# A product by seven block products for eight in two more pairs of feature blocks, with the order of the units written anew

## The chip, the cores and the metric

The kernel runs on one core of one Trainium2 chip. The metric is the device time of one execution in microseconds (us). Five engines work side by side, each through a queue of its own that it serves in order: TensorE (PE in the profile; PEld is its weight loads), VectorE (DVE), ScalarE (ACT), GpSimd (POOL) and SyncE (SP), which here only issues DMAs. The engines meet only at semaphores.

## The reference: what is computed

```python
# q, k, v: (4, 8, 768, 64); lam: (8,); blocks of 64 tokens, state kv carried from block to block
intra = ((qb @ kb.T) * Dmask) @ vb
inter = (qb * lam_pow) @ kv_state
out[block] = intra + inter
kv_state = lam**64 * kv_state + (kb * rev_pow).T @ vb
...
x = out.transpose(0, 2, 1, 3).reshape(3072, 512)
h = x @ w_in            # 512 -> 2048
g = np.maximum(0.01 * h, h)
y = g @ w_out           # 2048 -> 512
```

Everything is float32 to begin with (the launch hands the two weight matrices over as float64).

## The kernel before, in words

**Three passes for one product.** Each float32 operand is split into three parts, high, low and middle (`h`, `l`, `m`), and each product is three matmuls on TensorE. So an activation needs one ScalarE pass (`h`) and two VectorE passes (`l`, `m`) before TensorE can use it.

**Tokens and features.** The 3072 tokens are 24 chunks of 128; four chunks are a group of 512 tokens (six groups, `g` = 0 to 5), and two groups are a pair of groups (`pr` = 0, 1, 2). The 2048 features are 8 pairs of blocks of 128 (`p` = 0 to 7).

- *Attention* of chunk `c` is a round: `round_of` (transposes, `scores`, `outputs`), line 328 for its small matmuls, 418 for its transposes. It writes the group's `X[g % 2]`.
- *Weights in*: `w_in(p)` (line 639) loads 1 MB, puts float32 together from the two words (lines 603 to 610) and splits it (line 612) into `W[p]`.
- *Up*: `up(g, p)` (line 704) is X times `W[p]`: two blocks of 12 matmuls of 512 columns (line 716). ScalarE scales the bank between the second and third pass (line 734) and then applies the leaky ReLU into one of two `gs` buffers (line 739). From there the result goes to DRAM, as `G` (line 745) or, where the seven-product form is used, as `BB`: then `sums` (line 767) also makes three sums of quarters on VectorE, 128x256 each (line 773), and stores six quarter blocks for four (line 781), through a spare buffer that `spare` names (line 757).
- *Weights out*: `w_out` and `w_out_parts` bring `W_out` and put it in the place of `W[p]` after the last group's `up`; `w_sums(p)` (line 677) makes the sums of the weights' quarters that the seven-product form needs.
- *Out*: the activations come back from DRAM as *units* of 512 KB in a ring of five slots (`unit`, line 799): load on SP's queue (line 815), `h` on ScalarE (818), `l` and `m` on VectorE (821, 825). TensorE uses a unit in one of two ways. `plain(pr, p, gi)` (line 868) is 24 matmuls (line 841) for one group and one pair of feature blocks, into four banks. `strassen(pr, t, u)` (line 844) is 12 matmuls for block product `t` of seven, for a pair of groups and two pairs of feature blocks (`u`). Seven such units stand for eight times 12 matmuls. The price is in other places: unit 4 takes two loads and one more VectorE pass (833), and partial results are copied (`copy_banks`, 943) and added (`add_banks`, 948 and 949) between the accumulating banks X, Y, V and Z (two banks each).

**Before**, pairs of groups 1 and 2 use the seven-product form for `p` = 0 to 3 (`NS = 4`, two `u`), and pair 0 is all `plain`.

**The order.** The list `seq` (line 951 on) holds steps in order of rank. `Plan.add` takes each operation with an assumed cost, what it reads and writes, and that rank. `Plan.emit` (line 83) lists them: of all operations that are ready, it takes the one that can start earliest by the assumed costs, and among equals the one of lower rank. So an operation of TensorE that is ready goes ahead of one of lower rank that is late. Each engine's queue is then fixed in that order. `LEAD` puts the load and the split of a unit 8 steps ahead of its matmuls. The ring's first seven units use slots 0, 1, 4, 0, 1, 2, 3 (`slots`, line 797): 0 and 1 lie in `X[0]`, 2 and 3 in `X[1]`, which the last group's `up` reads, and 4 lies in `raws`.

Of the kernel before, what the change touches and what calls it, by code (L numbers as in the profile page):

```python
# [36 lines left out]
class Plan:  # L37
# [7 lines left out]
    def __init__(self):  # L45
        self.ops, self.last, self.rank = [], {}, 0.0
        self.chain, self.chains = None, {}
        self.warm, self.slack, self.more = 0.0, 0.0, {}
        self.first = {"PE": 0.0, "ACT": 0.0, "DVE": 3.4, "POOL": 0.0, "DMA": 0.2}
        self.cold, self.idle, self.spare = 6.0, None, None  # L50
# [10 lines left out]
    def add(self, eng, us, fn, reads=(), writes=(), rank=0.0):  # L61

        n, deps = len(self.ops), set()
        for k in reads:
            w, r = self.last.setdefault(k, [None, []])
            if w is not None:
                deps.add(w)
            r.append(n)
        for k in writes:
            w, r = self.last.setdefault(k, [None, []])  # L70
            if w is not None:
                deps.add(w)
            deps.update(r)
            self.last[k] = [n, []]
        deps.discard(n)
        ways = {eng: us} if isinstance(eng, str) else dict(zip(eng, us))
        if self.slack:
            self.more[n] = self.slack
        if self.chain is not None:
            self.chains[self.chain].append(n)  # L80
        self.ops.append((ways, fn, deps, (self.rank + rank, n), set(writes)))

    def emit(self):
# [30 lines left out]
        while len(done) < n:  # L114
            best = None
            for e in free:
                for i in able[e]:
                    if e == "PE" and (i != locked[0] if locked else i in follows):
                        continue
                    t = max(free[e], since(i, e))  # L120
                    if (best is None or (t, self.ops[i][3]) < best[:2]) and good(i, e, t):
                        best = (t, self.ops[i][3], i, e)
            t, _, i, e = best
            ways, fn = self.ops[i][:2]
# [38 lines left out]
def kernel(  # L163
# [10 lines left out]
    nc = tc.nc  # L174
# [23 lines left out]

    NS = 4
    LEAD = 8.0  # L200
    WSLACK = 5.0
    DV = 10
# [36 lines left out]
    KINDS_B = ("1", "7", "2", "3", "5", "6")  # L239
    BB = [[dram.tile([P, 6 * 2 * T], F32, name=f"b{r}_{u}", tag=f"b{r}_{u}") for u in range(NS // 2 if r else 0)] for r in range(NG // 2)]  # L240
    G = [{p: dram.tile([P, 4 * T], F32, name=f"g{r}_{p}", tag=f"g{r}_{p}") for p in range(NS if r else 0, NP)} for r in range(NG // 2)]


    NA = 9120
    att = sb([P, NA], "att")
    used = 0
# [7 lines left out]
    ident = part(P)  # L254
    kqv_f = [part(2 * H * D + (TURN - 2) * HP * C * (i == 1)) for i in range(3)]
    kqv = [[x[:, i * H * D:(i + 1) * H * D].rearrange("p (h d) -> p h d", h=H) for i in range(2)] for x in kqv_f]
# [389 lines left out]
    ATT = ["fk", "fq", "sc"] + [f"{x}{i}" for x in ("k", "q", "v", "kT", "qT", "qsT") for i in range(2)] + [f"st{i}" for i in range(4)]  # L646
    staging = [w32f, lowt.bitcast(F32), gs[1].rearrange("p f t -> p (f t)")]
# [3 lines left out]

    def free_attention():
        extra["att"] = sb([P, NA], "att", F32R)

# [9 lines left out]
    def more(z, p):  # L664
        a, n = (p * 3 + z) * 3 * NQ, 3 * NQ
        return extra["att"][:, a:a + n] if a + n <= NA else extra["lows"][:, :n]

# [36 lines left out]
    def up(g, p, lo=0, hi=GC):  # L704
# [20 lines left out]
        for fs in blocks:  # L725
            kb = ("b10", "b2")[n_b % 2] if n_b < 0 else ("b10", "b11", "b2")[n_b % 3]
# [6 lines left out]
            ns = 0.6 if len(fs) * n == T else 0.4  # L733
            add("ACT", ns, lambda b=b: nc.scalar.activation(out=b, in_=b, func=AF.Copy, bias=0.0, scale=S + 1.0), [], [kb], rank=-1.5)  # L734
            for i, f in enumerate(fs):
                add("PE", us, lambda f=f, d=b[:, i, :]: product(d, f, 2), keys("m"), [kb])
            for i, f in enumerate(fs if p < NS and g > 1 else [None]):
# [19 lines left out]
    def spare(g, p):  # L757

        r = raws.rearrange("p (i n) -> p i n", i=NRAW)
        if g == NG - 1:  # L760
            x, i = (kTs, qTs)[p // 2], p % 2
            return x[i].rearrange("p y t -> p (y t)").rearrange("p (i t) -> p i t", i=2), f"{'kq'[p // 2]}T{i}"
        if p % 2:
            return lows[1].bitcast(F32).rearrange("p (i t) -> p i t", i=2), "low1"
# [79 lines left out]
    def strassen(pr, t, u, lead):  # L844
# [20 lines left out]
        add("PE", 0.227 * 12, go, [f"r{z}{j}" for z in "hlm"] + [f"{'w' if w >= 0 else 'e'}{z}{p}" for z in "hlm" for p in ps_],  # L865
            ACC[d])

    def plain(pr, p, gi, lead, last=False, banks=None):
# [9 lines left out]
        def go(fs, cs, lo=0, n=T):  # L878
            for f in fs:
                for c in cs:  # L880
                    d, i = BANKS[gi][c]
                    product(acc[d][i][:, lo:lo + n], j, f * T + lo,
                            lambda z, f=f, c=c: W[p][z][:, f * 2 * NQ + c * P:f * 2 * NQ + (c + 1) * P], first=pr == p == f == 0, n=n)

# [60 lines left out]
    def add_banks(d, s):  # L945
        for i in range(2):
# [3 lines left out]

    seq = [("a", 0), ("a", 1), ("a", 2), ("a", 3), ("wi", 1), ("b", 4), ("r", 4), ("up", 0, 1), ("wi", 0), ("r", 5),
# [4 lines left out]
    nxt, n_out, begin = 3 * GC, 0, len(seq)  # L956
    ORDER = [4, 0, 5, 1, 6, 2, 7, 3]
    steps = [(g, p) for g in range(2, NG) for p in (ORDER if g < NG - 1 else range(NP))]

    def key_of(g, p):  # L960
        return f"G{g}{p}00" if p >= NS else f"B{g}{p}"

    for n, (g, p) in enumerate(steps):
# [10 lines left out]
        if g == NG - 1:  # L974
            seq.append(("wp", p))
            if p == NS - 1:
                seq.append(("fr",))
    for pr in range(NG // 2):
# [11 lines left out]
        else:  # L990
            i = seq.index(("up", NG - 1, NP - 1))
            seq[i:i] = [n(0, 0)]
            seq += [n(0, 1), n(1, 0), n(1, 1), ("ws", 0), n(2, 0), n(2, 1), ("ws", 1), n(3, 0), n(3, 1), ("ws", 2), n(4, 0), n(5, 0), ("ws", 3), n(6, 0), n(7, 0)]
    seq += [n(p, 1) for p in range(NS, NP - 2)] + [("end", NG // 2 - 1, 1, NP - 2)]

    freed = False
    for n, x in enumerate(seq):
# [9 lines left out]
        elif x[0] == "wi":  # L1007
            w_in(x[1])
        elif x[0] == "up":
            up(*x[1:])  # L1010
        elif x[0] == "wo":
            w_out(*x[1:])
        elif x[0] == "wp":
            if not freed:
                add("DVE", 0.0, lambda: None, [], ["psc", "po", "X0", "X1", "Z0", "Z1"])
                freed = True
            w_out_parts(x[1])
        elif x[0] == "ws":
            if x[1] == 0:
                add("DVE", 0.0, free_attention, [], ATT + [f"e{z}{p}" for z in "hlm" for p in range(NS)])  # L1020
            w_sums(x[1])
        elif x[0] == "fr":
            add("ACT", 0.0, free_raws, [], [f"raw{i}" for i in range(NRAW)] + ["rh4", "rl4", "rm4", "zr"])
        elif x[0] == "s":
            strassen(*x[1:], LEAD)
        elif x[0] == "n":
            plain(*x[1:], LEAD)
        elif x[0] == "copy":
# [38 lines left out]
```

## Time and profile before

| | |
|---|---|
| median of 3 runs | 600.31 us (599.99 to 600.97) |
| the profiled execution | 600.87 us |
| its span (first to last instruction) | 599.1 us |
| TensorE busy, instructions | 588.3 us, 5346 |
| VectorE / ScalarE / GpSimd busy | 393.8 / 290.6 / 132.3 us |
| granted TensorE clock | 1.000 |
| DMA | 119.89 MB, mean 200 GB/s |

The profile's times are from the span's start. Its parts that are used here: the busy time of each engine in stretches of 10 us; the list of who waited for whom; the time line of one engine (start, duration, line, operation, how often; in brackets the idle time before it and what ended it); and the mean duration of groups of instructions.

### The profile page before, as it was taken

The page shows a single profiled execution, that of the slowest core. Times are in us where ns is not written, and L with a number is a line of the kernel's source. Part 1 is how long each engine was busy: PE and PEld are TensorE (multiplying, and loading weights), DVE is VectorE, ACT ScalarE, POOL GpSimd, SP SyncE. Part 2 cuts the span into 40 slices and gives each one's busy share as a digit, 9 for nine tenths or more (in the row PEclk, how much of TensorE's full clock was granted, in tenths as well). Part 3 has the DMA queues.
Part 4 walks back from the last instruction along what each step waited for, and adds up shares of the span by engine and source line. Part 5 has one row for each costly group of instructions (what it writes and reads, how often), then busy time and mean ns, then how long its engine had stood idle before and what let it go on. Part 6 is the DMA issues. An engine that isn't in the chain of part 4 may idle for free.

```text
span 599.1 us, 13248 instructions
## 1 busy us (share of the span) xinstructions
PE 588.3 (98%) x5346; PEld 487.3 (81%) x5346; DVE 393.8 (66%) x534; ACT 290.6 (49%) x459; POOL 132.3 (22%) x170
## 2 busy tenths in 40 slices
PE   7899999999999999999999999999999999999997
PEld 6678888888888888888788888888888888888886
DVE  4999783434375664465279849876678695788752
ACT  3678975445555555565587744431344233252210
POOL 2554660554657374230000000000000000000000
PEclk9999999999999999999999999999999999999999
DMA  9899864795979999886678636436467546384533
GB/s 209 217 274 253 241 185 123 176 242 145 240 240 254 243 261 258 256 234 226 211 271 310 227 100 208 153 101 180 136 174 247 177 141 187 129 253 169 176 106 70
DMA packets 162797, 119.89 MB, mean 200 GB/s; under 512 B 100272, under 2 KB 139440, under 8 KB 162736
## 3 DMA queue, kind: packets, MB, share of 16 engines
q1 hardware_dynamic: 146976, 109.60, 62.4%
q10 hardware_dynamic: 13200, 5.77, 3.7%
q0 software_dynamic: 2560, 3.68, 2.4%
q8 instruction: 42, 0.69, 0.5%
q14 instruction: 19, 0.16, 0.1%
HBM read 79.17 MB, written 39.85 MB: 199 GB/s over the span
## 4 chain that ended last, share of the span: by engine, by line
PE 95%; DMA 2%; DVE 1%; ACT 0%; issue 0%; SPq 0%
PE b L716 44%; PE b L841 14%; PE po L841 13%; PE psc L841 11%; PE pt L841 5%; PE po L328 4%; PE psc L328 3%; DMA att<-in_k_dram 2%; PE pt L418 1%; DMA att<-in_q_dram 1%; PE po L418 0%; PE b L275 0%; DVE w L609 0%; ACT att L430 0%; DVE att L438 0%; DVE att L467 0%
## 5 line engine op out<-in xcount | busy, mean ns | idle before, releaser
L716 PE MATMUL b<-xh,wh 128*128 128x512 f32 (+2 forms) x392 | 103.5, 387 | 0.9 <-ACT xh L522 0.8
L716 PE MATMUL b<-xm,wm 128*128 128x512 f32 (+2 forms) x392 | 104.0, 392 | 0.0
L716 PE MATMUL b<-xl,wl 128*128 128x512 f32 (+2 forms) x392 | 103.2, 387 | 0.0
L818 ACT ACTIVATE xh<-xm 128x1024 fp32r<-128x1024 f32 x45 | 47.7, 1060 | 95.4 <-DMA xm<-g 44.1
L716 PEld LDWEIGHTS b<-xh,wh 128*128 128x128 f32 x392 | 72.8, 188 | 16.3 <-ACT xh L522 0.9
L716 PEld LDWEIGHTS b<-xl,wl 128*128 128x128 f32 x392 | 72.9, 188 | 14.8
L716 PEld LDWEIGHTS b<-xm,wm 128*128 128x128 f32 x392 | 71.5, 188 | 14.9
L734 ACT ACTIVATE b<-b 128x512 f32<-128x512 f32 (+2 forms) x97 | 56.2, 581 | 55.1 <-PE b L716 54.9
L739 ACT ACTIVATE gs<-b 128x512 f32<-128x512 f32 (+2 forms) x97 | 57.0, 591 | 48.9 <-PE b L716 40.8
L821 DVE SCALAR_TENSOR_TENSOR xl<-xm,xh 128x1024 fp32r<-128x1024 f32 x45 | 54.8, 1218 | 31.6 <-ACT xh L818 30.2
L825 DVE SCALAR_TENSOR_TENSOR xm<-xl,xh 128x1024 fp32r<-128x1024 f32 x48 | 58.7, 1224 | 3.3
L467 DVE TENSOR_TENSOR att<-psc,att 128x512 f32<-128x512 f32 x24 | 16.5, 689 | 47.4 <-PE psc L328 47.3
L477 POOL TENSOR_TENSOR att<-att 128x256 f32<-128x256 f32 x40 | 33.0, 826 | 38.3 <-DVE att L474 38.2
L438 POOL TENSOR_TENSOR att<-att 128x512 f32<-128x512 f32 (+1 forms) x20 | 25.3, 1265 | 72.3 <-PE po L328 50.4
L389 POOL DMA_DIRECT2D att<-in_q_dram x64 | 39.5, 623 | 2.7 <-DVE att L398 1.7
L610 DVE CUSTOM_DVE_ANT_0 w<-w,lows 128x1024 uint16<-128x1024 uint16 x32 | 31.6, 986 | 7.3 <-ACT lows L607 5.9
L609 DVE TENSOR_SCALAR w<-w 128x512 int32<-128x512 int32 x32 | 18.6, 580 | 25.1 <-ACT w L603 25.1
L328 PEld LDWEIGHTS po<-att 64*64 64x64 f32 x1472 | 27.1, 134 | 9.0 <-issue 6.1
L328 PE MATMUL po<-att 64*64 64x64 f32 x1472 | 32.9, 222 | 0.7 <-ACT att L506 0.3
L841 PE MATMUL b<-xh,wh 128*128 128x512 f32 (+1 forms) x88 | 33.5, 380 | 0.0
L841 PE MATMUL b<-xm,wm 128*128 128x512 f32 (+1 forms) x88 | 33.4, 379 | 0.0
L841 PE MATMUL b<-xl,wl 128*128 128x512 f32 (+1 forms) x88 | 33.4, 379 | 0.0
(152 smaller groups left out, 1045.8 us busy)
## 6 DMA issues: line engine op xcount, KB each, us to landing
g<-gs SPq DMA_DIRECT2D x31, 512.0 KB, 4.4
xm<-g SPq DMA_DIRECT2D x25, 512.0 KB, 4.2
xm<-b SPq DMA_DIRECT2D x23, 512.0 KB, 3.8
raws<-in_moe_w_in_dram SPq DMA_DIRECT2D x16, 512.0 KB, 5.4
raws<-in_moe_w_out_dram SPq DMA_DIRECT2D x16, 512.0 KB, 4.4
b<-gs SPq DMA_DIRECT2D x16, 512.0 KB, 4.1
att<-in_k_dram SPq DMA_DIRECT2D x48, 128.0 KB, 4.5
att<-in_v_dram SPq DMA_DIRECT2D x24, 256.0 KB, 4.7
```

The lines of the kernel that those rows point to most:

```text
L328: nc.tensor.matmul(dst[HALF[cols]], lhsT=lhsT[HALF[rows]], rhs=rhs[HALF[rows]], start=start, stop=True, skip_group_check=True)
L389: (move if nm == "k" else carry)(0.55 if nm == "k" else QSL, lambda o=o, z=z, e=nc.sync if nm == "k" else nc.gpsimd: e.dma_start(out=o.rea ...
L438: add(eng, us, lambda: e.tensor_tensor(o, x, _bc(pow_q, 2, 2)[:, :, m, :], op=ALU.mult), ["fq", dep], [f"qsT{i}"])
L477: add("POOL", 0.7, lambda new=new, j=j: nc.gpsimd.tensor_tensor(state[(j + 1) % 4], new, _bc(lam_c, 2, D), op=ALU.mult), [f"st{j % 4}", "f ...
L610: add("DVE", 1.0, lambda: nc.vector.tensor_tensor(d, d, low, op=ALU.add), [kl], [key])
L716: nc.tensor.matmul(dst, lhsT=w[z][:, kk * 2 * P + f * P:kk * 2 * P + (f + 1) * P], rhs=x[z][:, kk, toks], start=start and kk == 0, stop=kk ...
L734: add("ACT", ns, lambda b=b: nc.scalar.activation(out=b, in_=b, func=AF.Copy, bias=0.0, scale=S + 1.0), [], [kb], rank=-1.5)
L739: add("ACT", t, lambda o=o, x=s_: nc.scalar.activation(out=o, in_=x, func=AF.Prelu, bias=0.0, scale=(1.0 + 1.0 / S) / (WS * U), alpha=0.01 ...
L818: nc.scalar.activation(out=ring[j][0], in_=g(), func=AF.Copy, bias=0.0, scale=NEAR)
L821: nc.vector.scalar_tensor_tensor(ring[j][1], g(), 1.0, ring[j][0].bitcast(F32), op0=ALU.mult, op1=ALU.subtract)
L825: nc.vector.scalar_tensor_tensor(m, l.bitcast(F32), -S, h.bitcast(F32), op0=ALU.mult, op1=ALU.add)
L841: nc.tensor.matmul(dst, lhsT=lhs(z), rhs=ring[j][z][:, col:col + n], start=first and z == 0, stop=z == 2, skip_group_check=True)
```

## The change

Pair of groups 0 uses the seven-product form too, for `p` = 0 and 1 (`NS0 = 2`, one `u`). In detail:

- `up(g, 0)` and `up(g, 1)` of groups 0 and 1 go through `sums` into `BB`. Their spare buffers are free only after the last `w_in`, so the first stage of `seq` is in another order, which does these four late.
- In the output stage of pair 0, seven `strassen` units take the place of four `plain` ones, and the list is rewritten: `s(1,0)` and the copy of X into Z stand ahead of `up(5, 7)`, then `s(6)`, copy, `s(5)`, add, `s(7)`, add, `s(3)`, and `plain` and `strassen` units in turn. Behind `s(1,0)` come two matmuls of 256 columns into the two Z banks, which nothing has written in full before, and whose values the copy replaces.
- `w_sums(0)` and `w_sums(1)` move ahead to `up(5, 2)`, with `raw` buffers as staging; 2 and 3 stay in the output stage. For that the tile `att` is cut in two (`att`, `attb`), of which the first is given up earlier, and the last group's `sums` use one spare buffer (`qx`) in place of four.
- Banks of the `up` blocks turn by two (`TURN_B`), groups 2 to 4 take the pairs of features in another order (`ORDER`), the units of pair 0 have a lead of 12 (`LEAD0`), `w_out_parts` a rank 2 later (`WPR`), and ScalarE's operations in the last group's `up` are listed as if they could start 0.15 us earlier (`HOLD`).

```diff
+                    t = since(i, e)
+                    t, key = max(free[e], t), max(free[e], t - self.held.get(i, 0.0))
...
-    NS = 4
+    NS, NS0 = 4, 2
     LEAD = 8.0
+    TURN_B = 2
+    HOLD, WPR, WSR, LEAD0 = 0.15, 2.0, 0.0, 12.0
...
-    NA = 9120
-    att = sb([P, NA], "att")
+    NA, NB = 5536, 3584
+    att, att_b = sb([P, NA], "att"), sb([P, NB], "attb")
...
-        if p in (1, 2):
-            add("POOL", 0.0, lambda: None, [], [f"raw{3 - p}", "zr"], rank=-30.0)
...
-        j, jr, main, rest = SK[0], SK[1], staging[0], staging[1]
+        j, jr, main, rest = (SK[0], SK[1], staging[0], staging[1]) if p >= NS0 else (["raw1", "zr"], ["raw2"], raw[1], raw[2])
...
-        if p >= NS or g < 2:
+        if p >= (NS if g > 1 else NS0):
...
+            if begins:
+                for b in acc["Z"]:
+                    nc.tensor.matmul(b[:, HT:], lhsT=operand(0, 0, 0)[:, :P], rhs=ring[j][0][:, :HT], start=False, stop=True,
+                                     skip_group_check=True)
...
-    seq = [("a", 0), ("a", 1), ("a", 2), ("a", 3), ("wi", 1), ("b", 4), ("r", 4), ("up", 0, 1), ("wi", 0), ("r", 5),
-           ("wi", 2), ("wi", 3), ("up", 0, 0), ("up", 0, 2), ("up", 0, 3), ("r", 6), ("up", 1, 1, 0, 3), ("r", 7),
...
+    seq = [('a', 0), ('a', 1), ('a', 2), ('a', 3), ('wi', 5), ('b', 4), ('up', 0, 5), ('wi', 2), ('wi', 6), ('r', 4), ('r', 5), ('up', 0, 2), ('wi', 3), ('r', 6), ('up', 0, 6), ('r', 7), ('up', 0, 3), ('wi', 4), ('wi', 0), ('up', 0, 4), ('up', 1, 5, 0, 3), ('up', 1, 3), ('wi', 7), ('wi', 1), ('up', 1, 4), ('up', 0, 0), ('up', 1, 5, 3, 4), ('up', 1, 7), ('up', 0, 1), ('ls',), ('up', 1, 6), ('up', 0, 7), ('r', 8), ('up', 1, 0), ('lt',), ('r', 9), ('r', 10), ('r', 11), ('up', 1, 2), ('up', 1, 1)]
...
-    ORDER = [4, 0, 5, 1, 6, 2, 7, 3]
+    ORDER = [4, 0, 3, 7, 2, 6, 5, 1]
...
-            seq[i:i] = [n(0, 0)]
-            seq += [n(0, 1), n(1, 0), n(1, 1), ("ws", 0), n(2, 0), n(2, 1), ("ws", 1), n(3, 0), n(3, 1), ("ws", 2), n(4, 0), n(5, 0), ("ws", 3), n(6, 0), n(7, 0)]
+            put(("up", NG - 1, 2), ("ws", 0))
+            put(("up", NG - 1, 2), ("ws", 1))
+            put(("up", NG - 1, 6), ("fr",))
+            put(("up", NG - 1, 7), s(1, 0), ("copy", "Z", "X"))
+            seq += [s(6, 0), ("copy", "Y", "Z"), s(5, 0), ("add", "Y", "V"), s(7, 0), ("add", "V", "Z"), s(3, 0), n(2, 0), s(2, 0), n(3, 1), s(4, 0), n(2, 1), ("ws", 2), n(3, 0), ("ws", 3)]
+            seq += [n(p, 0) for p in range(NS, NP)]
```

More of the change, by code (lines that the diff above doesn't have):

```diff
@@ L48, in __init__ @@
         self.warm, self.slack, self.more = 0.0, 0.0, {}
+        self.ahead, self.held = 0.0, {}
         self.first = {"PE": 0.0, "ACT": 0.0, "DVE": 3.4, "POOL": 0.0, "DMA": 0.2}
@@ L78, in add @@
             self.more[n] = self.slack
+        if self.ahead:
+            self.held[n] = self.ahead
         if self.chain is not None:
@@ L119, in emit @@
                         continue
[L120 to L123, printed above, removed]
+                    t = since(i, e)
+                    t, key = max(free[e], t), max(free[e], t - self.held.get(i, 0.0))
+                    if (best is None or (key, self.ops[i][3]) < best[:2]) and good(i, e, t):
+                        best = (key, self.ops[i][3], i, e, t)
+            _, _, i, e, t = best
             ways, fn = self.ops[i][:2]
@@ L254 @@
     ident = part(P)
-    kqv_f = [part(2 * H * D + (TURN - 2) * HP * C * (i == 1)) for i in range(3)]
+    kqv_f = [att_b[:, lo:hi] for lo, hi in ((0, 2 * H * D), (2 * H * D, 4 * H * D + HP * C), (4 * H * D + HP * C, NB))]
     kqv = [[x[:, i * H * D:(i + 1) * H * D].rearrange("p (h d) -> p h d", h=H) for i in range(2)] for x in kqv_f]
@@ L650, with free_attention @@
     NQ = d_model // 2
-    def free_attention():
-        extra["att"] = sb([P, NA], "att", F32R)
+    def free_attention(x="att"):
+        extra[x] = sb([P, NA if x == "att" else NB], x, F32R)
     def free_lows():
@@ L736, in up @@
                 add("PE", us, lambda f=f, d=b[:, i, :]: product(d, f, 2), keys("m"), [kb])
-            for i, f in enumerate(fs if p < NS and g > 1 else [None]):
+            for i, f in enumerate(fs if p < (NS if g > 1 else NS0) else [None]):
                 o, s_, t = (r, b, ns) if f is None else (r[:, i, :], b[:, i, :], 0.2 + 0.4 * n / T)
@@ L741, in up @@
                     [kb], [f"gs{jg}"], rank=-1.5)
-        if p >= NS or g < 2:
+        plan.ahead = 0.0
+        if p >= (NS if g > 1 else NS0):
             d = G[g // 2][p].rearrange("p (f h g t) -> p f h g t", f=2, h=2, g=2)
@@ L760, in spare @@
         if g == NG - 1:
-            x, i = (kTs, qTs)[p // 2], p % 2
-            return x[i].rearrange("p y t -> p (y t)").rearrange("p (i t) -> p i t", i=2), f"{'kq'[p // 2]}T{i}"
-        if p % 2:
+            if p == 0:
+                add("POOL", 0.0, lambda: None, ["q0", "q1"], ["qx"])
+            return kqv_f[1][:, 4 * H * D - 2 * H * D:].rearrange("p (i t) -> p i t", i=2), "qx"
+        elif p % 2:
             return lows[1].bitcast(F32).rearrange("p (i t) -> p i t", i=2), "low1"
@@ L1008 @@
             w_in(x[1])
+            if not any(y[0] == "wi" for y in seq[n + 1:]):
+                add("POOL", 0.0, lambda: None, [], ["raw1", "raw2", "zr"], rank=-30.0)
         elif x[0] == "up":
@@ L1016 @@
                 freed = True
+            plan.rank += WPR
             w_out_parts(x[1])
@@ L1019 @@
             if x[1] == 0:
-                add("DVE", 0.0, free_attention, [], ATT + [f"e{z}{p}" for z in "hlm" for p in range(NS)])
+                add("DVE", 0.0, free_attention, [], ATT + [f"e{z}{p}" for z in "hlm" for p in range(2)] + ["el3"])
+            if x[1] == 2:
+                add("DVE", 0.0, lambda: free_attention("attb"), [], ATT_B + [f"e{z}2" for z in "hlm"] + ["eh3"])
+            plan.rank += WSR
             w_sums(x[1])
@@ L1024 @@
         elif x[0] == "s":
-            strassen(*x[1:], LEAD)
+            strassen(*x[1:], LEAD if x[1] else LEAD0)
         elif x[0] == "n":
-            plain(*x[1:], LEAD)
+            plain(*x[1:], LEAD if x[1] else LEAD0)
         elif x[0] == "copy":
```

31 lines of the change are left out of this document (18 added, 13 removed), and 3 rows, old and new, of the table seq.

## The prediction

> **What bounds the kernel now.** I read the page's busy shares first, then the busy time in stretches of 10 us, then who TensorE waited for.
>
> ```profile
> PE 588.3 (98%) x5346; PEld 487.3 (81%) x5346; DVE 393.8 (66%) x534; ACT 290.6 (49%) x459; POOL 132.3 (22%) x170
> PEclk9999999999999999999999999999999999999999
> ```
>
> ```profile
> 30.00:40.00 10.00, 9.89 (x106) 7.79 (x105) 9.25 (x13) 6.82 (x13) 6.25 (x6) 1.00 1.14 283
> ...
> 300.00:310.00 10.00, 10.00 (x45) 8.28 (x45) 6.35 (x11) 8.31 (x14) 0.00 (x0) 1.00 0.69 227
> 310.00:320.00 10.00, 10.00 (x45) 8.26 (x44) 9.40 (x14) 8.23 (x14) 0.00 (x0) 1.00 1.03 376
> 320.00:330.00 10.00, 10.00 (x46) 8.28 (x45) 9.49 (x14) 6.11 (x10) 0.00 (x0) 1.00 0.81 284
> ```
>
> The columns are length, PE, PEld, DVE, ACT, POOL, clock, DMA share, GB/s. From 50 us to 590 us TensorE is busy 10.00 of 10.00 in every stretch but one (290 to 300: 9.72), at the full clock. Of the 10.8 us in which it is idle, 5.75 lie in the first 30 us, 0.34 between 30 and 50, 0.28 near 293, and 4.4 behind the last matmul. So the time is the start (until the first `up` matmul at 29.45), plus TensorE's work, plus the end. A matmul fewer shows in full, and so does any new wait on TensorE, since no slack is left for it.
>
> **What the change removes.** In the chain of work that ended last, `1.36 PE psc L841 x6` is 226.7 ns for one output matmul of 512 columns. Pair 0 has 8 x 2 `plain` units of 24, which are 384 matmuls. After: 7 x 12 + 12 x 24 = 372. That is 12 x 0.2267 = **-2.72 us**. The two added matmuls of 256 columns start 0.12 us apart in the time line (591.55, 591.66, 591.78): **+0.24**. Net -2.48.
>
> The Trainium skill, page "TensorE: Matmul & The Clock Gate", section "Back-to-back issue gap", gives about 131 ns for a 512-column matmul in a sustained stream with weight loads, and 215.7 ns on its own. By these the twelve would be worth 1.57 or 2.59 us; this trace has 226.7 at the full clock, so it does not bear out the first.
>
> **What it adds off TensorE.**
> - `sums` four more times: three VectorE operations of 0.42, 0.43 and 0.42 us, 5.1 us in all, between 85 and 150 us. VectorE is busy 4.46, 1.88, 5.70, 4.73 and 0.53 of 10 in the five stretches from 90 us, so at nothing; if it were late, the two `gs` buffers would hold ScalarE's line 739 and with it a bank. Stores grow by 4 x 256 KB; the DMA share there is 0.43 to 0.91.
> - Units: 7 + 12, three more, and one more load in unit 4, so four loads of 512 KB. VectorE: 3 x (1.22 + 1.23) + 1.22 for line 833 + four additions of 0.69 = 11.3 us. ScalarE: 3 x 1.06 + four copies of 0.57 and four of 0.58 = 7.8. VectorE is busy 91.5 us of the 120 from 300 to 420 us; 102.8 of 117.5 is 87%. It fits as a sum, so at nothing there; the places where it may not fit in time are below.
> - `w_sums(0)` and `(1)` are moved, not added. Each is 4.45 us on VectorE (four of 0.42, then 0.42, 0.96, 0.43 and 0.96) and 2.5 on ScalarE (0.41, 0.83, about 0.38 and 0.85). They leave 343 to 370 us and come to about 300 to 330.
> - Cutting `att` in two, the bank turn and the order of groups 2 to 4 add no instruction. TensorE was fed without a gap from 72 to 291 us with ScalarE at 3.8 to 8 of 10, and I see no reason for a change there: 0.
>
> **What may wait: the ring.** Units now last 2.72 us on TensorE where they lasted 5.44, so a slot must be filled again in half the time. A slot is free when its unit's last matmul is done; then come load, line 818, lines 821 and 825. From the time line of pair 1:
>
> ```profile
> 425.82 5.76 SPq L815 DMA_DIRECT2D xm<-b  x2
> ```
>
> ```profile
> 429.79 1.06 ACT L818 ACTIVATE xh<-xm 128x1024 fp32r<-128x1024 f32 x1 [1.82 <-DMA xm<-b]
> ```
>
> ```profile
> 430.88 1.23 DVE L821 SCALAR_TENSOR_TENSOR xl<-xm,xh 128x1024 fp32r<-128x1024 f32 x1 [0.32 <-ACT xh L818]
> 432.21 1.23 DVE L825 SCALAR_TENSOR_TENSOR xm<-xl,xh 128x1024 fp32r<-128x1024 f32 x1
> ```
>
> From 425.82 to 433.44 is 7.6 us. The load issued at 444.86 was ready at 454.99, after 10.1 us, with a slower landing. In the new order the slots are s(1): 0, s(6): 1, s(5): 4, s(7): 0, s(3): 1. So s(3) waits for the slot of s(6), and slots 2 and 3 for the end of `up(5, 7)`. What covers it is s(5) and s(7), 5.44 us, and what is left of `up(5, 7)` when s(6) runs. Before, the third unit of pair 0 was taken ahead of the last 0.91 us piece of `up(5, 7)`:
>
> ```profile
> 348.56 0.39 PE L841 MATMUL psc<-raws,wh 128*128 128x512 f32 x1
> ...
> 354.00 1.07 PE L716 MATMUL b<-xm,wm 128*128 128x512 f32 x4
> ```
>
> and the first unit of pair 0 went in at 325.90, three `up` steps ahead of its place, when ScalarE was late. Three cases: s(6) goes in with four pieces left (cover 9.1 us, wait 0 to 1.0); with one left (6.35, wait 1.2 to 3.8); after all (5.44, 2.2 to 4.7). Both ends are -0 and +4.7. I take **+0.6**, the middle of the first case: the first unit was ready at 323.8 and taken at 325.9, and the list takes whatever is ready at the first gap, so s(1) and s(6) can go in early; four of the five loads are also asked for 12 steps ahead now.
>
> **The adds and copies.** s(7) needs Y filled from Z, s(3) needs V added into Y: two ScalarE copies of 0.58 and two additions of 0.69, some 2.2 us with the hand-overs, behind one unit of 2.72 us where pairs 1 and 2 have two. It fits by 0.5 us if ScalarE and VectorE take them at once; a 1.22 us operation of VectorE ahead of them makes it 0.7 us late, at each of two places. Bounds 0 to 1.4; I take **+0.2**, since in pair 1 the additions at 448.56 began 0.4 us after their ScalarE copy ended.
>
> **The start.** VectorE is busy 9.25 to 9.63 of 10 from 20 to 60 us and makes a `W[p]` ready every 8 to 11 us (line 636 ends at 30.1, 40.9, 49.5, 58.9 and 68.8). The new list asks for the second and third weights ahead of rounds 4 and 5, and brings in group 1 after five distinct weights instead of four. The work per weight is the same, so 0; bounds -0.6 (all that is idle after 30 us) to +2 (one round late by the 2 us that its VectorE part lasts).
>
> **Sum.** -2.72 + 0.24 + 0.6 + 0.2 = -1.7 us. Against the profiled execution (600.87, span 599.1, 1.8 around it) that is 599.2 and a span of 597.4. It lies 0.56 above the median of the runs, so against the median I say **598.6**.
>
> **Rivals.**
> 1. *The ring takes it back.* One unit too late by 2 to 4.7 us, once, at s(3) or the `plain` unit behind it. For it: three of the first five units reuse slots at half the distance in time. Against it: pairs 1 and 2 alternate units in the same ring with no gap at all. Gain 2.48 less 2.0 to 4.7: 599.8 to 602.5, around 600.6. Chance 0.2.
> 2. *Slower: VectorE and ScalarE overflow in the last group's `up`.* From 300 to 330 us VectorE is busy 25.2 of 30 and ScalarE 22.7; two `w_sums` make 34.1 and 27.7, so VectorE runs over by 4.1 us unless other work goes out. If what is pushed out is the `sums` of this group, the `gs` buffers stay full, ScalarE cannot empty a bank, and TensorE stops; s(1), the only filler, itself needs both `w_sums`. +4.1 gives 600.31 - 2.48 + 4.1 = 601.9. It decides from 3.7 us of such waits (2.48 + 1.2). Against it: `w_out_parts` (2.5 us of VectorE each) now rank later and give way, and units stand later too. Chance 0.13.
>    The Trainium skill, same page, section "What's actually happening", says that an idle window of about 3.4 us halves the clock until a busy one has passed; such a stop would then cost some 1.7 us more. No wait after 30 us here is over 0.28 us, and the clock is 1.00 in each stretch, so the trace can't show it.
> 3. *The start moves.* Within the bounds above and with the rest as forecast: 598.0 to 600.6. Chance 0.1.
> 4. *The full gain*: no wait at all, and the idle of 0.23 at 41.7 and 0.28 at 293 gone: 600.31 - 2.48 - 0.5 = 597.3. Chance 0.17.
>
> The forecast itself (598.0 to 599.2) has 0.4. That the change does not do what it says can be left out: the twelve matmuls are counted in the loops.
>
> **Chances.** 0.2% is 1.2 us, about what a measurement of this kernel can tell from no change: faster is below 599.1, slower above 601.5. Faster: 0.36 of the forecast, 0.17 of case 4, 0.05 of case 3: 0.58. Slower: 0.06 of case 1, 0.12 of case 2, 0.01 of case 3: 0.19. Same: the rest, 0.23. The range runs from case 4 to inside case 2, 596.9 to 601.8; under 2 in 10 is left out.
>
> **What the changed profile would show.** 12 fewer matmuls of 512 columns on line 841 and two new ones of 256. TensorE at 10.00 in each stretch from 300 to 400 us if the forecast holds; a wait "PE ... <- DVE xm L825" (or the new lines' numbers) of 1 us or more near 350 us for rival 1, a wait on ScalarE's lines 734 or 739 between 300 and 345 us for rival 2. The first `up` matmul near 29.5 us and no idle over 0.5 us from 30 to 75 us if the start is unmoved. I am wrong in the mechanism if TensorE's busy time does not fall by about 2.5 us, or if it falls and the span does not although no wait is seen.

## The result, and the profile after

| | before | after |
|---|---|---|
| median of 9 runs each, taken together | 600.96 us (599.82 to 601.54) | 598.85 us (598.53 to 599.53) |
| ratio, 95% interval | | 0.9971 [0.996, 0.9981] |
| the profiled execution, its span | 600.87, 599.1 us | 598.83, 597.1 us |
| first matmul of `up` | 29.45 us | 28.32 us |
| last group of attention matmuls begins (a) | 291.51 us | 291.07 us |
| from (a) to TensorE's last matmul: the *stretch* | 303.15 us | 301.56 us |
| behind the last matmul | 4.42 us | 4.42 us |

The kernel is faster by 0.29%. The first line of the page, busy time by engine, and its clock:

```profile
PE 586.2 (98%) x5336; PEld 485.0 (81%) x5336; DVE 406.7 (68%) x559; ACT 299.2 (50%) x468; POOL 134.0 (22%) x170
PEclk9999999999999999999999999999999999999999
```

TensorE's busy time fell by 2.1 us and VectorE's rose by 12.9. The busy time in stretches of 10 us (columns as in the prediction), with one row of before that was not shown there, from 350 to 360:

```profile
350.00:360.00 10.00, 10.00 (x46) 8.29 (x45) 3.19 (x4) 3.71 (x5) 0.00 (x0) 1.00 0.39 117
```

and after:

```profile
30.00:40.00 10.00, 9.34 (x103) 7.15 (x103) 9.24 (x13) 8.69 (x15) 5.84 (x5) 1.00 1.06 285
300.00:310.00 10.00, 10.00 (x45) 8.28 (x45) 7.67 (x12) 9.14 (x14) 0.00 (x0) 1.00 0.84 266
310.00:320.00 10.00, 10.00 (x45) 8.26 (x44) 8.79 (x17) 8.52 (x15) 0.00 (x0) 1.00 0.99 339
320.00:330.00 10.00, 10.00 (x46) 8.21 (x45) 9.83 (x15) 8.86 (x14) 0.00 (x0) 1.00 0.75 238
...
350.00:360.00 10.00, 9.88 (x43) 7.82 (x43) 8.19 (x10) 7.51 (x11) 0.00 (x0) 1.00 0.98 316
360.00:370.00 10.00, 10.00 (x45) 8.26 (x44) 9.61 (x9) 3.62 (x4) 0.00 (x0) 1.00 0.57 197
```

VectorE and ScalarE are fuller from 300 to 330 us, and TensorE still has its 10.00. From 300 us on only 350 to 360 shows a gap. A matmul's record lasts 0.39 us where the next starts after 0.227, so a delay under 0.16 us counts as busy and these columns can't show it. TensorE's time line has the gap at the `m` part of the `plain` unit behind s(3) (line 851 was 841, 723 was 716):

```profile
323.68 0.39 PE L851 MATMUL psc<-xh,wh 128*128 128x512 f32 x1
...
326.40 0.40 PE L878 MATMUL po<-xh,wh 128*128 128x256 f32 x2
...
332.10 0.39 PE L851 MATMUL po<-xh,att 128*128 128x512 f32 x1
...
357.76 0.39 PE L851 MATMUL psc<-xl,wl 128*128 128x512 f32 x1
358.27 0.50 PE L851 MATMUL psc<-xm,wm 128*128 128x512 f32 x1
358.61 0.40 PE L851 MATMUL psc<-xh,wh 128*128 128x512 f32 x1
```

The first three lines are s(1), the two matmuls of 256 columns, and s(6). s(1) and s(6) have gone in between the pieces of `up`, ahead of their place in `seq`. From 357.76 to 358.27 is 0.51 us where 0.227 is the rule: a wait of 0.29. The matmul that waited lasts 0.50 in place of 0.39, and its successor starts 0.34 later: another 0.11. The chain of work that ended last names the cause:

```profile
339.97 9.14 PE b L723 x41
349.11 5.50 DMA xm<-g
...
354.64 1.07 ACT xh L828
...
355.73 1.24 DVE xl L831
...
356.99 1.24 DVE xm L835
...
358.27 1.21 PE psc L851 x4
```

That is the ring (pieces of 0.02 to 0.04 us are left out): the slot comes free with the end of `up(5, 7)`, in this chain at 349.1, and 9.1 us later the unit is ready.

**Where the 1.59 us of the stretch come from.** Spacing by spacing, from the start of one matmul to the next: 12 matmuls of 512 columns fewer and two of 256 more are -2.48 (301.08 to 298.60). Delays above 0.06 us went from 0.20 to 0.60: the ring wait and its restart, +0.40. Delays below 0.06 us each went from 0.33 to 0.81: +0.48. Together -1.60.

Two thirds of those small delays have a place. Each of the six seven-product units of pairs 1 and 2 that take a part of their weights' sums from `attb`, the tile that was cut off `att`, is 0.054 us longer than its twelve matmuls, most of it in the seven that begin it:

```profile
436.88 1.78 PE L851 MATMUL po<-raws,attb 128*128 128x512 f32 x7
438.50 0.39 PE L851 MATMUL po<-raws,att 128*128 128x512 f32 x1
```

These seven take 1.62 us from start to start where 1.59 is usual, and the first of them starts 0.006 late. Six units are 0.32 us. The same six are as long in every run with the cut `att`, e13 among them; before, where these sums lay in `att` and `lows`, the same units lose nothing. Why weights from `attb` cost it is not shown.

The rest of the span's -2.0 is the start, 0.44 us earlier at (a). A second profiled execution of the changed kernel had its first `up` matmul at 29.59, (a) at 292.86 and a stretch of 301.74; so a start that differs by 1.8 us between two executions of one program says nothing of the change. The experiments are therefore compared by the stretch, and by the ratio of the medians beside it. A stretch is that of one profiled execution each; the two of the changed kernel differ by 0.18 us.

### The profile page after: what moved, and what is told of

The parts are those of the page before. It is cut to its first block, busy times and chain, and to the rows that moved or that the text cites. A ratio compares the mean times of both kernels' runs of the same rounds, so it can differ in the third digit from the quotient of the medians.

```text
span 597.1 us, 13281 instructions
## 1 busy us (share of the span) xinstructions
PE 586.2 (98%) x5336; PEld 485.0 (81%) x5336; DVE 406.7 (68%) x559; ACT 299.2 (50%) x468; POOL 134.0 (22%) x170
## 4 chain that ended last, share of the span: by engine, by line
PE 91%; DVE 5%; DMA 2%; ACT 0%; issue 0%; SPq 0%; DVEq 0%
PE b L723 43%; PE po L851 13%; PE b L851 12%; PE psc L851 11%; PE pt L851 4%; PE po L335 4%; PE psc L335 3%; DMA xm<-g 1%; DVE wl L628 1%; DVE w L617 1%; DMA attb<-in_q_dram 1%; DVE w L616 1%; PE pt L425 1%; DVE att L474 0%; DVE xl L530 0%
## 5 line engine op out<-in xcount | busy, mean ns | idle before, releaser
L835 DVE SCALAR_TENSOR_TENSOR xm<-xl,xh 128x1024 fp32r<-128x1024 f32 x50 | 61.2, 1224 | 3.5
L484 POOL TENSOR_TENSOR att<-att 128x256 f32<-128x256 f32 x40 | 34.9, 873 | 37.9 <-DVE att L481 37.9
L616 DVE TENSOR_SCALAR w<-w 128x512 int32<-128x512 int32 x32 | 22.6, 706 | 27.2 <-ACT w L610 27.1
L396 POOL DMA_DIRECT2D attb<-in_q_dram x64 | 39.5, 624 | 2.9 <-issue 1.4
L441 POOL TENSOR_TENSOR attb<-attb,att 128x512 f32<-128x512 f32 (+1 forms) x23 | 26.1, 1136 | 34.6 <-PE po L425 10.5
L851 PE MATMUL psc<-xm,wm 128*128 128x512 f32 x84 | 32.8, 391 | 0.1
L851 PE MATMUL psc<-xh,wh 128*128 128x512 f32 x84 | 32.7, 389 | 0.0
L851 PE MATMUL psc<-xl,wl 128*128 128x512 f32 x84 | 32.7, 389 | 0.0
L617 DVE CUSTOM_DVE_ANT_0 w<-w,lows 128x1024 uint16<-128x1024 uint16 x32 | 26.2, 818 | 7.1 <-ACT lows L614 6.2
L828 ACT ACTIVATE raws<-raws 128x1024 fp32r<-128x1024 f32 x12 | 12.7, 1061 | 27.6 <-DMA raws<-g 18.1
```

Source lines behind the costliest of these rows:

```text
L396: (move if nm == "k" else carry)(0.55 if nm == "k" else QSL, lambda o=o, z=z, e=nc.sync if nm == "k" else nc.gpsimd: e.dma_start(out=o.rea ...
L484: add("POOL", 0.7, lambda new=new, j=j: nc.gpsimd.tensor_tensor(state[(j + 1) % 4], new, _bc(lam_c, 2, D), op=ALU.mult), [f"st{j % 4}", "f ...
L616: add("DVE", 0.42, lambda: nc.vector.tensor_scalar(d, d, 3, None, op0=ALU.logical_shift_left), [], [key])
L617: add("DVE", 1.0, lambda: nc.vector.tensor_tensor(d, d, low, op=ALU.add), [kl], [key])
L828: nc.scalar.activation(out=ring[j][0], in_=g(), func=AF.Copy, bias=0.0, scale=NEAR)
L835: nc.vector.scalar_tensor_tensor(m, l.bitcast(F32), -S, h.bitcast(F32), op0=ALU.mult, op1=ALU.add)
```

## The experiments

**The same kernel again** (e0), with the ratio and the spread of a repeat.

> The changed kernel again, beside the next three on the same chip: 598.5 to 599.5 us, a ring wait of 0.2 to 0.4 us at the plain unit behind s(3).

Ratio 0.9966 [0.9952, 0.9979], stretch 301.74. The ring wait of 0.47 is above the 0.2 to 0.4 that was expected. The median of 599.99 is too, but so is that of before beside it, 601.76.

**Pair 0 all `plain`, everything else new** (e1).

```diff
-    NS, NS0 = 4, 2
+    NS, NS0 = 4, 0
...
-            put(("up", NG - 1, 7), s(1, 0), ("copy", "Z", "X"))
+            put(("up", NG - 1, 7), n(0, 0))
```

> Undoes one part: pair 0 is all plain units again (384 + 720 matmuls of 512 columns on the output line), with the steps of that pair in the order of the kernel before, while the new order of the start, of groups 2 to 4 and of the banks, the 0.15 us of preference and the cut of att stay. My theory (the gain is the matmuls that are not done, 2.48 us net, less a ring wait of 0.3 to 0.5 us at the eighth-product unit's successor): this is 2.0 us slower than the changed kernel, about 600.9 us, no different from the kernel before (ratio 0.998 to 1.002); from the last attention matmul to TensorE's last 303.1 us, as before, against 301.6 in the changed kernel. Rival (the new order of the rest is what gains): 598.9 us, 301.6 us in that stretch.

(The steps of pair 0 are in the old order too, with all four `w_sums` behind the last `up`.) Ratio 1.0196 [1.018, 1.0212], stretch 305.57, 2.5 above the 303.1 that was expected. The 1.96% are not the price of the matmuls: TensorE runs into a wait ahead of (a), for a transpose on VectorE that itself waits for loads of `q`. The time lines of TensorE and VectorE, and the busy times there:

```profile
149.38 0.49 PE L335 MATMUL psc<-att 64*64 64x64 f32 x8 [5.75 <-DVE att L405]
...
151.01 3.78 PE L723 MATMUL b<-xh,wh 128*128 128x512 f32 x8 [0.72 <-ACT xh L529]
```

```profile
149.01 0.50 DVE L405 STREAM_TRANSPOSE att<-lows 128x128 f32<-128x128 f32 x2 [5.60 <-DMA lows<-in_q_dram]
```

```profile
146.00:150.00 4.00, 0.62 (x24) 0.63 (x24) 0.57 (x3) 0.00 (x0) 0.54 (x1) 0.56 0.55 136
150.00:154.00 4.00, 3.28 (x19) 2.52 (x12) 3.94 (x8) 0.60 (x1) 2.77 (x5) 0.50 0.01 2
154.00:158.00 4.00, 4.00 (x39) 2.90 (x41) 0.87 (x4) 1.47 (x3) 1.69 (x3) 0.66 0.37 74
```

The changed kernel has this start order with the `sums`, e13 below has neither, and neither of them has the wait. So it takes the new order without the `sums`; why the loads then come late was not tried. After 5.75 us without work the granted clock (the seventh column) is 0.50, and the next eight matmuls stand 0.45 us apart (3.58 us from 151.01 to the next group) where 0.227 is usual. The prediction had said that the trace of before could not show what a long wait does to the clock. Here it is seen: the clock is 1.00 from 142 to 146 us, 0.56 on average from 146 to 150, and 1.00 again from 158 on, so it fell during the wait and stayed at a half until about 156.8. From 151.0 to 156.8 us that is an estimated 2.9 us lost. The Trainium skill, page "TensorE: Matmul & The Clock Gate", section "What's actually happening", says that an idle window of about 3.4 us halves the clock; these rows agree. The 1.7 us that the prediction worked out from the Trainium skill for such a stop, beside the wait, is less than the 2.9 of these rows. The run as a whole is no test of the twelve matmuls, so it was made again with the old start.

**Pair 0 all `plain` and the start as before: the rest of the change alone** (e13).

```diff
-    NS, NS0 = 4, 2
+    NS, NS0 = 4, 0
...
-    seq = [('a', 0), ('a', 1), ('a', 2), ('a', 3), ('wi', 5), ('b', 4), ('up', 0, 5), ('wi', 2), ...
+    seq = [("a", 0), ("a", 1), ("a", 2), ("a", 3), ("wi", 1), ("b", 4), ("r", 4), ("up", 0, 1), ...
...
-            put(("up", NG - 1, 7), s(1, 0), ("copy", "Z", "X"))
+            put(("up", NG - 1, 7), n(0, 0))
```

> Pair 0 with its sixteen plain units as before and with the start as before, and the rest of the change kept: the order of groups 2 to 4, the turn of the banks, the earlier listing of ScalarE's operations, the later rank of the weights out, the lead of 12 and the cut of att. Theory, that the gain comes from the matmuls alone: no gain; the stretch is 303.1 us as before, or up to 305.6 with the two waits of e1 (0.83 and 0.91) again, and the time is 1.000 to 1.004 of the kernel before. Rival, that the new order of the rest brings the gain: the stretch is 301.6 and the time 0.997.

(The place of the `w_sums` and the freeing of the `raw` buffers are as before too.) Ratio 1.0016 [1.0001, 1.0031], stretch 304.30. In this order four matmuls of `up` stand ahead of (a) that stand behind it in the others; with their 0.91 us the stretch that compares is 305.21, within 0.4 of e1's 305.57. No gain, then, as expected: the rest by itself costs 2.06 us of the stretch. The profile names one wait of it, on ScalarE's last leaky ReLU of `up` (line 749 there):

```profile
356.05 0.49 PE L853 MATMUL b<-xh,wh 128*128 128x512 f32 x1 [0.75 <-ACT gs L749]
```

The spacing there is 0.92 us too long. All delays above 0.06 us are 1.59 in place of before's 0.20. Those below are 0.96, 0.32 of them at the six units with `attb`, so they come with the rest and not with the seven-product form. From this kernel to the changed one the stretch falls by 3.65 (3.47 by the second execution): 2.48 are the matmuls, 1.0 are delays that are gone where the seven-product units stand in their place, 0.15 are small ones. That the units cover them is read from the order and was not tried by itself.

**ScalarE's operations not listed early** (e6).

```diff
-    HOLD, WPR, WSR, LEAD0 = 0.15, 2.0, 0.0, 12.0
+    HOLD, WPR, WSR, LEAD0 = 0.0, 2.0, 0.0, 12.0
```

> HOLD is 0: the list takes s(5) ahead of the last 0.91 us piece of up(5, 7) and not behind it; TensorE's matmuls are the same in number. Ring theory: the plain unit behind s(3) sits in a slot that is free only when up(5, 7) has read X[1], and took 9.1 us from there in the changed kernel; the cover from there is now s(7) and s(3), 5.44 us, where it was 8.16. So TensorE waits 3.0 to 3.7 us at that unit instead of 0.28: 2.7 to 3.4 us slower than the changed kernel, 601.5 to 602.3 us, a little slower than the kernel before. Rival (TensorE's work alone sets the time; the order within it does not matter): 598.9 us and no wait over 0.5 us.

Ratio 1.0022 [1.0004, 1.004], stretch 305.46, +3.9 over the changed kernel. TensorE's waits in its time line:

```profile
354.34 0.50 PE L851 MATMUL po<-xh,att 128*128 128x512 f32 x1 [1.35 <-ACT b L960]
...
360.27 0.49 PE L851 MATMUL psc<-xh,wh 128*128 128x512 f32 x1 [0.19 <-ACT xh L828]
...
361.52 0.49 PE L851 MATMUL psc<-xl,wl 128*128 128x512 f32 x1 [0.77 <-DVE xl L831]
...
362.78 0.51 PE L851 MATMUL psc<-xm,wm 128*128 128x512 f32 x1 [0.76 <-DVE xm L835]
```

The three waits on slot 2's `h`, `l` and `m` are the late ring unit (0.35, 1.03 and 1.03 us by the spacings: 2.4). The first is a bank copy that now has no unit between it and the last piece of `up` (1.51). The ring wait was expected at 3.0 to 3.7; the copy was not, and by its 1.51 the ring's load has more time. The two less the changed kernel's own 0.29 make 3.6 of the 3.9. The ratio is 0.5% above the changed kernel's.

**The sums of the weights four steps later** (e4).

```diff
-            put(("up", NG - 1, 2), ("ws", 0))
-            put(("up", NG - 1, 2), ("ws", 1))
+            put(("up", NG - 1, 6), ("ws", 0))
+            put(("up", NG - 1, 6), ("ws", 1))
```

> The weights' sums of pairs 0 and 1 stand ahead of up(5, 6) and not of up(5, 2). s(1) then goes in one and a half up steps later, and s(6) only 1.81 us ahead of the end of up(5, 7). Ring theory: s(3) waits for the slot of s(6); the cover is 1.81 + 5.44 = 7.25 us against 7.6 to 10.1 us from slot to unit, a wait of 0.4 to 2.9 us there, which then covers the 0.28 us at the next unit. Time 599.0 to 601.5 us, 600.2 in the middle. Rival (VectorE and ScalarE are the limit between 300 and 350 us, and late sums relieve them): no slower than the changed kernel, 598.5 to 598.9 us.

Ratio 1.0042 [1.002, 1.0065], stretch 306.96, +5.4. That is twice what either theory allowed. From 320 to 340 us TensorE waits five times. One of them, the operation of ScalarE that it waits for, and the busy times:

```profile
329.70 1.21 PE L723 MATMUL b<-xm,wm 128*128 128x512 f32 x4 [0.67 <-ACT b L742]
```

```profile
329.06 0.58 ACT L742 ACTIVATE b<-b 128x512 f32<-128x512 f32 x1 [3.12 <-PE b L723]
```

```profile
320.00:330.00 10.00, 8.94 (x38) 6.66 (x37) 9.31 (x13) 6.59 (x11) 0.00 (x0) 1.00 0.58 198
330.00:340.00 10.00, 8.71 (x35) 6.07 (x34) 7.50 (x14) 6.81 (x13) 0.00 (x0) 1.00 0.71 238
```

The waits are always for ScalarE's passes over the `up` banks, 3.2 us together by the spacings; the remaining ones are 0.85 at s(3) and 0.82 on a copy. The later sums do relieve both engines: ScalarE is busy 6.59 and 6.81 of 10 where the changed kernel has 8.86 and 8.68, VectorE 9.31 and 7.50 where it has 9.83 and 9.00. It does not help. ScalarE is not overloaded here: it stood idle for 3.12 us, itself waiting for TensorE, just ahead of the pass that TensorE then waits for. TensorE's third pass over a bank needs ScalarE's in between, a new block needs a bank that ScalarE has emptied, and with the sums late s(1) is not ready: it runs at 340.26 us, in the changed kernel at 323.68. So TensorE has no other matmuls to do meanwhile. That s(1) and s(6) would fill these waits is read from the order of the two kernels; the list of the other engines changed with the edit too.

**The banks not turned** (e5).

```diff
-    TURN_B = 2
+    TURN_B = 0
```

> The banks of the up blocks turn by 0: the last block of up(5, 7) lies in b11, which s(5) needs, so s(7) stands ahead of s(5), and s(7) needs Y filled from Z, which needs the other two banks emptied. Theory (banks): behind the last up piece TensorE waits for a ScalarE pass and two copies, 0.9 to 1.4 us, and the wait of 0.28 us at the plain unit behind s(3) goes, since its load has that much more time: 0.6 to 1.1 us slower than the changed kernel, 599.4 to 600.0 us. Rival (the bank turn does nothing, as I priced it in the prediction): 598.9 us and no wait behind the last up piece.

Ratio 1.0024 [1.0007, 1.004], stretch 304.08, +2.5. The profiled execution is the fastest of ten (600.09 us, the median is 602.72), so the stretch may understate the loss. The time lines of TensorE and of VectorE:

```profile
356.42 0.50 PE L851 MATMUL b<-xh,att 128*128 128x512 f32 x1 [1.65 <-DVE b L966]
```

```profile
354.53 1.22 DVE L831 SCALAR_TENSOR_TENSOR xl<-xm,xh 128x1024 fp32r<-128x1024 f32 x1 [2.89 <-ACT xh L828]
355.67 1.29 DVE L966 TENSOR_TENSOR b<-b,w 128x512 f32<-128x512 f32 x2
```

In this order s(5), whose banks are added into Y, stands directly ahead of s(3), which adds to Y. ScalarE's copies begin at 354.40, the additions get VectorE only behind a 1.22 us pass, and TensorE is 1.82 us late. In the changed kernel s(7) stands between the two and covers it. The wait of 0.82 at s(7) was expected, at 0.9 to 1.4; the 1.82 was not.

**s(2) ahead of the `plain` unit** (e7), to give the late unit 2.72 us more, **the same with the ring's slots 2 and 3 kept apart in the bookkeeping** (e9), and **that bookkeeping alone** (e10).

```diff
-            seq += [..., s(3, 0), n(2, 0), s(2, 0), n(3, 1), ...
+            seq += [..., s(3, 0), s(2, 0), n(2, 0), n(3, 1), ...
```

```diff
+        if first and j == 2:
+            for z in "hlm":
+                add("POOL", 0.0, lambda: None, [], [f"x{z}{j // 2}{cc}" for cc in range(GC)] + [f"r{z}{j // 2 * 2 + i}" for i in range(2)], rank=-30.0)
...
-            return [f"r{z}{j}"] + ([f"x{z}{j // 2}{cc}" for cc in range(GC)] if first and j < 4 else [])
+            return [f"r{z}{j}"] + ([f"x{z}0{cc}" for cc in range(GC)] if first and j < 2 else [])
```

> s(2) and the plain unit behind s(3) change places, in the list and so in the ring (s(2) in slot 2, the plain unit in slot 3). Ring theory with SP's queue in order: s(2) is asked for when up(5, 7) ends and lands sooner, so the wait of 0.28 us at the place behind s(3) goes; but the load of slot 3 stands in SP's queue behind a load that waits for the end of s(5), about 3.8 us after the slot is free, and with 7.6 to 10.1 us from there the plain unit, needed 11.1 us after the end of up(5, 7), is ready after 11.4 to 13.9: a new wait of 0.3 to 2.8 us. 598.9 to 601.2 us, 599.9 in the middle. Rival (a slot is loaded as soon as it is free): 0.3 to 0.45 us faster than the changed kernel, 598.5 us.

> As the swap before, and the list no longer makes the load of slot 3 wait for that of slot 2 (they shared bookkeeping keys, not memory), so it stands in SP's queue ahead of the load that waits for s(5), behind only the last store of up. Ring theory: slot 3 is asked for about 2 us after up(5, 7) ends, and the unit is ready 9.6 to 12.1 us after it, against 11.1 when TensorE gets there; both waits go or stay under 0.3 us: 0.2 to 0.45 us faster than the changed kernel, 598.4 to 598.7 us. Rival (what remains at that place is not the ring): as the changed kernel, 598.9 us.

> The changed kernel's own order of units with the keys mended alone: the load of slot 3 comes ahead of that which waits for s(5). Ring theory: the unit in slot 2 waits as before or a little longer (0.28 to 0.8 us), because a second load now shares its way, and s(2) in slot 3 was just in time and now has room: no gain, 598.8 to 599.4 us. Rival (earlier loads are all that counts): 598.5 us.

e7: ratio 1.0022 [1.0003, 1.004], stretch 303.45: worse by 1.9, with a new wait inside the 0.3 to 2.8 that were expected. Its twelve executions run from 601.03 to 606.51 us, and the profiled one (601.10) is among the fastest; the profile can't say what the long ones lost. The `plain` unit now takes slot 3, and the time line of SP's queue shows why it is late:

```profile
352.71 0.58 SPq L825 DMA_DIRECT2D raws<-g  x1
353.34 0.62 SPq L825 DMA_DIRECT2D xm<-g  x1
```

Its load leaves at 353.34 although its slot is free when `up(5, 7)` ends (TensorE's next unit starts at 349.79). It stands in the queue behind the load into `raws`, which must wait for the end of s(5) at 352.5. TensorE waits 1.03 for `l` and 1.03 for `m`. In e9 the load leaves at 350.98, the wait is 0.85, stretch 302.10, ratio 0.9962 [0.995, 0.9974]; in e10 the ring wait is 0.55, one of 0.71 appears at 321 us, stretch 302.63, ratio 0.996 [0.9946, 0.9975]. Neither is better than the changed kernel's 0.9966 [0.9952, 0.9979] beside them. For e10 that was expected; for e9 a gain of 0.2 to 0.45 us was.

**s(2) left out, in pair 0 (e11) and in pair 1 (e12)**, to see what twelve matmuls fewer are worth at each place.

```diff
-            for i, p in enumerate(ps_):
+            for i, p in enumerate(() if (pr, t, u) == (0, 2, 0) else ps_):
```

> The changed kernel with the twelve matmuls of s(2,0) of pair 0 left out (that block product of the output is missing); its unit is still loaded and split. Theory, that in pair 0 the ring and VectorE are at their limit just behind it (n(3,1) has its m ready at 364.2 us and s(4) its unit at 370.5, and VectorE is busy 9.6 of 10 from 360 to 380): only part of the 2.72 us of TensorE comes back, the stretch from the last attention group to TensorE's end falls by 1.2 us (1.0 to 1.9), and new waits of 0.8 to 1.7 us appear behind n(3,1). Rival, that TensorE alone sets the end: the stretch falls by 2.7 us and no new wait is seen.

> The changed kernel with the twelve matmuls of s(2,0) of pair 1 left out (that block product of the output is missing); its unit is still loaded and split. Theory, that pairs 1 and 2 have units ready well ahead and TensorE alone sets the end there: the stretch falls by 2.6 us (2.4 to 2.72). Rival, that the ring is as tight there as in pair 0: 1 to 1.9 us.

In pair 1 the stretch is 298.81: -2.75 against 301.56, the full price (2.4 to 2.72 was expected). In pair 0 it is 301.07: -0.5 (-0.7 against the second execution). The list of waits of e11:

```profile
PE b L851 <- DVE raws L835: 1.0, 1, 1.0
PE po L851 <- DVE xm L835: 0.4, 1, 0.4
PE psc L851 <- DVE xm L835: 0.3, 1, 0.3
```

By the spacings these are 1.21, 0.53 and 0.49, with three restarts of 0.11: 2.56 of delay where the changed kernel has 0.40. So a part is taken back, as the theory has it, but more of it than its range allowed (a fall of 1.0 to 1.9, new waits of 0.8 to 1.7). One difference is seen: the load into `raws` took 7.0 us from issue to landing where the changed kernel's profile has 5.9 and its second execution 6.5. With s(2) gone nothing covered that. How much of the 2.56 would stand with a load of 5.9 us is not known. The ratios, 0.9935 [0.992, 0.995] and 0.9924 [0.9907, 0.9942], do not tell the two apart, since the starts of these executions differ by a microsecond.

## Why the prediction was right, and what in it was not

The direction and the main term are right, and the runs bear them out. That the size came out within some 0.1 us of the forecast gain (-1.7, measured -1.6 over the stretch) is in part luck: one term that was set to 0 cost 0.48, and two others came out 0.4 smaller.

- **The matmuls, -2.72 + 0.24.** Right: 12 lines of 512 columns fewer, two of 256 more, and 226.7 ns each. e12 shows that twelve are worth 2.75 us where nothing else is late, and pair 0 in the seven-product form brings 3.65 against e13, more than its matmuls. The sign that was named for a wrong mechanism, TensorE's busy time not falling by about 2.5 us, needs a word: it fell by 2.1, since delays under 0.16 us, 0.48 more than before in all, count as busy.
- **The ring, +0.6.** Right in cause, and near in size (0.40 with the restart, 0.58 in the second execution), but for another unit. The three cases are worked out for s(3), which waits for the slot of s(6). s(6) went in at 332.10 us, with 64 matmuls of `up` left, sixteen pieces and not four; so s(3) did not wait at all. The wait stood at the `plain` unit behind it, which rival 1 names. Its slot is free only with the end of `up(5, 7)`, however early s(6) goes in, and its cover is s(5), s(7) and s(3), 8.16 us. The prediction names that slot but does not work it out: by its own 7.6 to 10.1 us the wait would have been 0 to 1.9. So the 0.6 (it is called the middle of 0 to 1.0, which is 0.5) came near by luck. e6 shows what less cover for this slot does, 2.4 us. The cover hangs on `HOLD`.
- **The adds and copies, +0.2.** No wait at all in the changed kernel. The bound of 1.4 holds with one unit of cover. Where that unit is moved, e5 has 1.82 + 0.82 and e6 1.51 at these very places. The mechanism of the 1.82, a 1.22 us pass of VectorE ahead of the additions, is the one named; the other two are ScalarE's copies into Y behind its last passes over the `up` banks.
- **Cutting `att`, the bank turn, the new orders: 0.** Wrong in size, and the step that was mis-sized most. e13 says that the rest alone costs 2.06 us of the stretch: 1.4 of delays in and behind the last `up`, which are absent in the changed kernel, and 0.6 of small ones, most of which stay. The changed kernel pays +0.48 of them. Of these, 0.32 sit at the six units that read weights from `attb`: the cut of `att`, counted as adding no instruction and so as 0, is what these have in common. What causes them there, and the rest of the small delays, is open. The +0.48 and the two terms that came out smaller (0.2 and 0.2) nearly cancel: sum -1.7, measured -1.59.
- **The start, 0.** Nothing can be said: 0.44 us earlier in the pair of profiles, later in the second, and 1.8 between two executions of one program. The idle time of TensorE from 30 to 60 us rose from 0.34 to 1.10, with a first `up` matmul 1.1 earlier; one wait of it is 0.67 us, over the 0.5 that was named as a sign that the start moved.
- **`sums` at nothing.** Right: 60.00 of 60 us busy from 90 to 150 us, with VectorE at 28.3 (23.6 before).
- **VectorE and ScalarE totals.** 16.4 us of new VectorE work were counted and 12.9 measured. The new instructions have the lengths that were taken (`sums` aside, 0.42 to 0.50), but the old ones changed. Line 617 (610 before) went from 986 to 818 ns a time, which is 5.4 us less in all, and line 616 from 580 to 706, 4.0 us more; and three passes of line 625 (618 before), 0.8 us each, went to ScalarE. The traces show where the means come from. GpSimd's time line and VectorE's, before:

```profile
34.41 1.05 POOL L434 TENSOR_TENSOR att<-att 64x512 f32<-64x512 f32 x1 [0.93 <-POOL att L434]
```

```profile
34.51 1.51 DVE L610 CUSTOM_DVE_ANT_0 w<-w,lows 128x1024 uint16<-128x1024 uint16 x1
```

The line's instructions that overlap no tensor operation of GpSimd last 0.68 to 0.69 us, in both kernels. All that last over 0.7 overlap one: 14 of 32 before, 6 of 32 after. So the mean falls with the number of such meetings.

- **Rival 2, overflow in the last group's `up`.** Did not happen: VectorE 26.3 of 30 from 300 to 330 us, ScalarE 26.5, TensorE full. e4 has waits on the very lines that it named, 3.2 us of them, but with the sums *late* and with ScalarE and VectorE less busy. So they are no overflow: the units that the sums feed are missing as filler.
- **Rival 4, the full gain**, failed by the ring wait and the small delays.

The forecast of 598.6 hangs on the old median of 600.31: times the ratio it is 598.6; the median measured beside the runs of before, whose own median is now 600.96, is 598.85, inside the 598.0 to 599.2 of the forecast.

## What to carry to other kernels

Count the matmuls that go, then ask at each unit behind them who covers its load, split and add: here 2.5 us of gain stood against 3.9, 5.4 and 2.5 us that one constant or one place in the list would have cost. Units that need nothing but their own data are worth most where TensorE must wait for another engine between two of its passes, so what makes them ready early is not overhead. An engine that is less busy does not help if its next pass still comes late (e4). Where the start of a program moves by more than the change is worth, measure from a fixed event behind it.

## What the runs showed of the hardware

- A matmul that has waited costs more than its wait: it lasts 0.50 us in the records in place of 0.39, and the next one starts 0.11 us late, at nearly every wait above 0.2 us in these runs.
- During a wait of 5.75 us the granted clock fell to 0.50, and it was back at 1.00 only by 158 us, some 7 us after the wait (e1).
- A load that is ready to go leaves up to 3.5 us late behind one that waits in the same queue (e7).
- A slot of the ring took 9.1 us from free to ready in the changed kernel's profile, of which the DMA was 5.5; the load into `raws` took 5.9 and 6.5 us in two executions of it, and 7.0 in e11.
- One VectorE instruction of one shape (line 610, then 617) lasts 0.68 to 0.69 us where it overlaps no tensor operation of GpSimd, and up to 2.20 us where it does.
- Matmuls whose weights lie in `attb` cost six units 0.054 us each; from `att` and `lows` the same units lose nothing.
